# Token rows in their own segment's step, heads in two halves: a recurrent attention loop that streams its weights

## The chip, the cores and the metric

The kernel runs on one core of a Trainium2 chip. Its metric is the device time of one execution in microseconds (us). The core has a matrix engine (PE, whose weight loads are told apart as PEld), a vector engine (DVE), a scalar engine (ACT), GpSimd (POOL) and SyncE (SP), and 16 DMA engines that all DMA queues share. Each engine works through its own list of instructions in order and waits on semaphores. Here SP issues the weight loads, POOL and ACT issue the other transfers of this part.

## The reference

Two independent parts are computed and put side by side. Part A is attention with a recurrent memory, part B a long convolution by FFT (part B's code is the same in both kernels). Part A, cut to what matters:

```python
# x: (1, 2048, 1024), mem0: (1, 8, 1024); 32 heads of 128; 64 segments of 32 tokens
mem = mem0
for s in range(n_seg):
    h = concatenate([mem, xs], axis=1)          # 8 memory rows + 32 token rows
    q, k, v = h @ Wq, h @ Wk, h @ Wv            # each 1024 x 4096
    scores = where(mask, q k^T * scale, -1e9)   # memory rows see all, tokens see causally
    o = softmax(scores) v
    o = einsum('bhte,hed->btd', o, Wo)          # 4096 x 1024
    mem = o[:, :M, :]                           # the next segment's memory
    outs.append(o[:, M:, :])                    # this segment's output
```

Only the 8 memory rows go from one segment to the next. All values are bf16.

## The kernel before, in words

Part B runs first, then `part_a`. The four weight matrices of part A are 64 units of 128 x 2048 bf16 (512 KB each): 8 chunks of the contraction (`kc`) by two halves of the heads (`t`) for each of k, q and v, and 16 units `u` of two heads each for Wo. They do not all fit on chip. 41 units stay there (`load_res`, L92), the others are loaded anew in every step (`unit`, L97) through a pool `wst` of four buffers: `STREAM` (L43) names 3 of every 8 units of k, q and v, `STREAM_O` (L44) 5 of the 16 of Wo. SP issues these loads in the order of use; the load for a buffer waits until PE has read the unit that was in it.

A prologue (L105 to L165) transposes x and projects the last 8 token rows of every segment, since 8 + 32 = 40 rows do not fit the 32-row tiles. Their k, q and v go to DRAM (`PKd`, L148 and L160) and come back segment by segment (`load_pk`). The 8 rows are called the left rows here.

The loop (L208) has 66 passes, s = -1 to 64, in manual order: the instructions stand on each engine in the order in which the code records them. Pass s works on a tile `hT` of 32 rows: the 24 other token rows of segment **s + 1** and the 8 memory rows of segment **s**. It

- projects k, q and v of these rows (`quads`, four 32-row groups of PE's columns at a time), transposes k and q (`tr`), and scores the rows that are due in pass s: memory rows of s with the token rows of s that pass s - 1 prepared (L316), and the left rows (L318);
- takes the softmax of all heads at once on DVE and ACT (`softmax_a`, `softmax_b`, `ptrans`), spreads the memory rows' probabilities into block form (`blocks`, L330, DVE) and forms probabilities times v (`pv`, L344), copied to `oT` (L345);
- projects with Wo: L353 for the 32 rows of `oT` (memory rows of s, token rows of s), and L358 a second pass over the same units for the left rows `oTL` of s - 1. `po` goes to `osb` (L371), its memory rows are transposed into the next `hT` (L379, L380);
- finishes the token rows' and left rows' probabilities on POOL and DVE beside that, for the next pass (L361 to L384), and stores the output of s - 1 in eight small DMAs from POOL (L388, L389).

Of the kernel before, what the change touches and what calls it, by code (L numbers as in the profile page):

```python
# [17 lines left out]
NEG = -1.0e9  # L18
# [5 lines left out]
def part_a(ctx, tc, x, mem0, Wq, Wk, Wv, Wo, seg_len, out_a):  # L24
# [12 lines left out]
    scale = float(E ** -0.5)  # L37

# [4 lines left out]
    STREAM = {(m, t, kc) for m in "kqv" for t in range(2) for kc in (2, 5, 7)}  # L43
    STREAM_O = (2, 5, 8, 11, 14)  # L44
# [8 lines left out]
    wres = ctx.enter_context(tc.tile_pool(name="a_wres", bufs=1))  # L53
    wst = ctx.enter_context(tc.tile_pool(name="a_wst", bufs=4))
    dram = ctx.enter_context(tc.tile_pool(name="a_dram", bufs=1, space=bass.MemoryType.DRAM))
    XTd = dram.tile([NS, 128, KC * XM], BF16, name="XTd")
    PKd = dram.tile([NS, 128, 768], BF16, name="PKd")

    ctx.enter_context(tc.manual_schedule())

    ident = const.tile([128, 128], BF16, name="a_ident")
    make_identity(nc, ident[:])
    maskS = const.tile([128, NK], BF16, name="maskS")
    maskL = const.tile([128, NK], BF16, name="maskL")
    nc.gpsimd.memset(maskS[:], 0.0)
    nc.gpsimd.memset(maskL[:], 0.0)
# [4 lines left out]
    mmem = const.tile([128, 1], F32, name="mmem")  # L71
    mx_ = const.tile([128, 1], F32, name="mxx")
    nc.gpsimd.memset(mmem[:], 1.0)
    nc.gpsimd.memset(mx_[:], 1.0)
    for g in range(4):
        p = slice(32 * g, 32 * g + 32)

        def keep(t, base, cm, pattern, fill):
            nc.gpsimd.affine_select(out=t, in_=t, compare_op=ALU.is_ge, fill=fill, base=base, pattern=pattern, channel_multiplier=cm)
        keep(maskS[p, 0:XM], 0, 1, [[-1, XM]], NEG)  # L80
        keep(maskS[p, SL:NK], -XM, 1, [[0, XL]], NEG)
        keep(maskL[p, SL:NK], 0, 1, [[-1, XL]], NEG)
        keep(mmem[p, :], -XM, 1, [[0, 1]], 0.0)
        keep(mx_[p, :], XM - 1, -1, [[0, 1]], 0.0)
# [7 lines left out]
    def load_res(key):  # L92
        t_ = wres.tile([128, 2048], BF16, name="W_%s" % "_".join(str(i) for i in key))
# [11 lines left out]
    with tc.tile_pool(name="a_pxl", bufs=1) as pxl, \  # L105
# [56 lines left out]
        for u in range(16):  # L162
            if u not in STREAM_O:
                load_res(("o", u))
        pro_cm.__exit__(None, None, None)  # L165

    pers = ctx.enter_context(tc.tile_pool(name="a_pers", bufs=1))
    ld = ctx.enter_context(tc.tile_pool(name="a_ld", bufs=2))
    work = ctx.enter_context(tc.tile_pool(name="a_work", bufs=1))
    ps_acc = ctx.enter_context(tc.tile_pool(name="a_acc", bufs=2, space=PSUM))  # L170
    ps_tr = ctx.enter_context(tc.tile_pool(name="a_tr", bufs=2, space=PSUM))
    ps_att = ctx.enter_context(tc.tile_pool(name="a_att", bufs=3, space=PSUM))
    ps_o = ctx.enter_context(tc.tile_pool(name="a_o", bufs=1, space=PSUM))

    KT = pers.tile([128, 8, 4, NK], BF16, name="KT")
    QT = pers.tile([128, 8, 4, SL], BF16, name="QT")
    V = [pers.tile([128, 8, 128], BF16, name=f"V{i}") for i in range(2)]
    oT = pers.tile([128, 8, 4, SL], BF16, name="oT")
    oTL = pers.tile([128, 8, 4, XL], BF16, name="oTL")
    for t_ in (KT, QT, oT, oTL):  # L180
        nc.vector.memset(t_[:], 0.0)

    po = ps_o.tile([128, 2, 256], F32, name="po", tag="po")
    nc.vector.memset(po[:], 0.0)

    def load_pk(j):
        pk = ld.tile([128, 768], BF16, name="pk", tag="pk")
# [3 lines left out]
    def load_xt(j):  # L191
        xt = ld.tile([128, KC, XM], BF16, name="xt", tag="xt", bufs=1)
# [574 lines left out]
```

## Time and profile before

| what | value |
|---|---|
| three runs | 4604.3, 4592.44, 4604.17 us (median 4604.17) |
| profiled execution | 4595.0 us, its span 4593.3 us |
| PE busy, share of the span | 3077.3 us, 67% |
| DVE, ACT, POOL busy | 1597.9, 1325.4, 890.2 us |
| part B, up to about | 1367 us |
| part A's prologue | 1367 to 1744 us |
| the loop of 66 passes | 1744 us to the end |
| mean granted TensorE clock | 0.812 |
| `wst` loads | 1513 of 512 KB each |

The page gives busy time by engine, the span in 40 slices, the DMA queues, the chain of work that ended last, the costliest groups of instructions with the idle time before them and what ended it, and the DMA issues with their time to landing. A table by stage (busy times of a window) has these columns after the window: its length, PE, PEld, DVE, ACT and POOL busy with the count of instructions, the granted clock (PEclk), the DMA engines' share and GB/s. A row of the timeline has start, duration, engine, line, operation, output<-inputs, shape and count, and in brackets the idle time of the engine before it and what ended it.

### The profile page before, as it was taken

To read this page: it belongs to the slowest core of one execution; us is meant where nothing else is said; L and a number is where in the kernel's file an instruction comes from. 1 tells how busy PE (TensorE), PEld (TensorE's weight loads), DVE (VectorE), ACT (ScalarE), POOL (GpSimd) and SP (SyncE) were. 2 spreads that over 40 slices of the span, in tenths; PEclk is the share of its full clock that TensorE was granted. 3 is DMA by queue.
4 is the path that set the end of the run, shared out by engine and by line. 5 is a ranking of instruction groups with operands and counts; after the bars stand their busy time and mean duration, and the time that the engine had idled before them with its cause. 6 is when DMAs were issued, how large, how long until landed. Compare 5 with 4: busy or idle time off the path is not lost.

```text
span 4593.3 us, 101731 instructions
## 1 busy us (share of the span) xinstructions
PE 3077.3 (67%) x44894; PEld 1597.2 (35%) x44990; DVE 1597.9 (35%) x2887; ACT 1325.4 (29%) x1962; POOL 890.2 (19%) x1493
## 2 busy tenths in 40 slices
PE   5555543499994675766777667666666766676666
PEld 2333322244432222333333333333333333333333
DVE  8888889543001111222222222222222222222221
ACT  7999999400000001111111111111111111111111
POOL 0000000033110041222222222222222222222222
PEclk8677765699996888788787878887888888878888
DMA  3111100443233547888888888888888888888887
GB/s 112 62 62 62 62 37 6 112 152 126 87 96 117 152 149 261 272 294 285 276 285 271 301 270 289 293 281 283 281 282 295 287 278 293 281 281 299 275 291 243
DMA packets 400811, 969.45 MB, mean 211 GB/s; under 512 B 108512, under 2 KB 117728, under 8 KB 400368
## 3 DMA queue, kind: packets, MB, share of 16 engines
q1 hardware_dynamic: 330144, 923.01, 59.1%
q0 software_dynamic: 26624, 24.18, 1.7%
q10 hardware_dynamic: 43600, 15.75, 1.4%
q8 instruction: 351, 5.75, 0.5%
q14 instruction: 92, 0.75, 0.0%
HBM read 898.72 MB, written 64.04 MB: 210 GB/s over the span
## 4 chain that ended last, share of the span: by engine, by line
PE 37%; DMA 36%; ACT 11%; DVE 10%; issue 3%; POOL 1%; SPq 0%; ACTq 0%; POOLq 0%; DVEq 0%
DMA wst<-in_A_Wv_dram 11%; DMA wst<-in_A_Wq_dram 11%; DMA wst<-in_A_Wk_dram 10%; PE acc L222 7%; PE po L353 6%; PE po L358 6%; PE yp L687 5%; PE Kc L657 3%; PE Ks L658 2%; DVE lb L282 2%; PE pk_l L156 2%; DMA PKd<-kst 2%; ACT sn L407 1%; DMA xb<-in_A_x_dram 1%; ACT E L532 1%
## 5 line engine op out<-in xcount | busy, mean ns | idle before, releaser
L222 PE MATMUL acc<-wst,hT 128*32 128x512 bf16 x4680 | 542.4, 450 | 658.8 <-DMA wst<-in_A_Wk_dram 269.6
L222 PEld LDWEIGHTS <-hT 128*32 128x32 bf16 x12480 | 368.9, 103 | 1253.8 <-issue 1084.6
L228 ACT CAST qk<-acc 128x512 bf16<-128x512 f32 x195 | 114.3, 586 | 1150.6 <-PE acc L222 1150.6
L353 PE MATMUL po<-W_o,oT 128*32 128x256 bf16 x5720 | 423.0, 320 | 29.8 <-ACT oT L345 29.5
L358 PE MATMUL po<-W_o,oTL 128*8 128x256 bf16 x5632 | 416.3, 318 | 0.6 <-ACT oTL L384 0.4
L561 PE MATMUL kps<-Fr,Gr 128*64 128x17 bf16 (+1 forms) x2048 | 119.9, 198 | 301.6 <-DVE Fr L554 301.4
L353 PEld LDWEIGHTS <-oT 128*32 128x32 bf16 x8320 | 252.7, 113 | 163.0 <-ACT oT L345 92.5
L222 PE MATMUL acc<-W_q,hT 128*32 128x512 bf16 x2600 | 286.4, 507 | 0.0
L228 DVE CAST qk<-acc 128x512 bf16<-128x512 f32 x65 | 45.0, 692 | 631.8 <-PE acc L222 631.8
L200 POOL COPY KT<-pk 128x256 bf16<-128x256 bf16 x64 | 25.1, 392 | 1226.5 <-PE sc L248 1224.2
L222 PE MATMUL acc<-W_v,hT 128*32 128x512 bf16 x2600 | 256.3, 434 | 0.0
L358 PEld LDWEIGHTS <-oTL 128*8 128x8 bf16 x8192 | 221.2, 100 | 43.8 <-issue 2.0
L222 PE MATMUL acc<-W_k,hT 128*32 128x512 bf16 x2600 | 221.3, 395 | 15.5 <-POOL hT L197 15.5
L561 PEld LDWEIGHTS <-Gr 128*64 128x64 bf16 x2048 | 108.0, 144 | 345.8 <-DVE Fr L554 305.6
L657 PE MATMUL Kc<-KT,Mc 128*128 128x512 bf16 (+1 forms) x544 | 207.4, 381 | 17.0 <-DMA KT<-Kdram 15.8
L388 POOL DMA_DIRECT2D out_dram<-osb x256 | 135.8, 531 | 395.4 <-DVE osb L371 382.7
L687 PE MATMUL yp<-Ycs,Mci 128*128 128x512 bf16 (+1 forms) x543 | 207.2, 382 | 5.5 <-DMA Mci<-Mdram 3.5
L658 PE MATMUL Ks<-KT,Ms 128*128 128x512 bf16 (+1 forms) x523 | 199.1, 381 | 0.0
L687 PE MATMUL yp<-Ycs,Msi 128*128 128x512 bf16 (+1 forms) x523 | 199.0, 381 | 0.1
L353 PE MATMUL po<-wst,oT 128*32 128x256 bf16 x2600 | 195.4, 315 | 0.1
L604 PE MATMUL Us<-u_sb,Ms 128*128 128x512 bf16 (+1 forms) x520 | 168.0, 422 | 40.7 <-ACT Ms L592 32.5
L373 ACT CAST osb<-po 128x256 bf16<-128x256 f32 x64 | 23.8, 372 | 583.5 <-DVE osb L371 583.5
(201 smaller groups left out, 5738.0 us busy)
## 6 DMA issues: line engine op xcount, KB each, us to landing
wst<-in_A_Wk_dram SPq DMA_DIRECT2D x396, 512.0 KB, 5.9
wst<-in_A_Wq_dram SPq DMA_DIRECT2D x396, 512.0 KB, 6.0
wst<-in_A_Wv_dram SPq DMA_DIRECT2D x396, 512.0 KB, 5.9
wst<-in_A_Wo_dram SPq DMA_DIRECT2D x325, 512.0 KB, 5.6
Udram<-Ucs SPq DMA_DIRECT2D x32, 512.0 KB, 2.7
Ucs<-Udram SPq DMA_DIRECT2D x32, 512.0 KB, 3.7
pk<-PKd POOLq DMA_DIRECT2D x64, 192.0 KB, 6.1
Mdram<-Ms SPq DMA_DIRECT2D x17, 544.0 KB, 2.7
```

The costliest lines, as they stand in the source:

```text
L156: nc.tensor.matmul(pk[:], lhsT=us[kc][:, 512 * g + 128 * hl:512 * g + 128 * hl + 128], rhs=xTl[:, kc, :, :].rearrange("p s k -> p (s k)"), ...
L222: nc.tensor.matmul(a[32 * g:32 * g + 32, :], lhsT=hT[:, kc, :], rhs=w[:, 512 * g:512 * g + 512], start=(kc == 0), stop=(kc == KC - 1), til ...
L228: (nc.scalar.copy if eng == "a" else nc.vector.tensor_copy)(out=q[:], in_=a[:])
L282: eng.tensor_tensor(out=lb[:], in0=bc(pl[:, t, q0:q1].unsqueeze(1), [128, 16, n]), in1=bc(BDL[:].rearrange("p a b -> p (a b)").unsqueeze(2 ...
L353: nc.tensor.matmul(po[32 * qt:32 * qt + 32, 0, :], lhsT=oT[:, th, g, :], rhs=w[:, 1024 * hh + 256 * qt:1024 * hh + 256 * qt + 256], start= ...
L358: nc.tensor.matmul(po[32 * qt:32 * qt + XL, 1, :], lhsT=oTL[:, th, g, :], rhs=w[:, 1024 * hh + 256 * qt:1024 * hh + 256 * qt + 256], start ...
L388: nc.gpsimd.dma_start(out=out_a[r0:r0 + XM, 256 * qt:256 * qt + 256], in_=osb[32 * qt:32 * qt + XM, 0, :])
L561: nc.tensor.matmul(kps[pp0:pp0 + 64, dd, 0:ncol], lhsT=Gr[:, dd, :], rhs=Fr[:, dd, par_i:I:2], start=True, stop=False, tile_position=(0, p ...
L604: nc.tensor.matmul(Us[0:MM, :], lhsT=Ms[:, lc, 0:MM], rhs=u_sb[:, lc, dsl], **st)
L657: nc.tensor.matmul(Kc[0:MM, :], lhsT=Mc[:, lc, 0:MM], rhs=KT[:, lc, dsl], **st)
L658: nc.tensor.matmul(Ks[0:MM, :], lhsT=Ms[:, lc, 0:MM], rhs=KT[:, lc, dsl], **st)
L687: nc.tensor.matmul(yp[:], lhsT=Mx[0:KK, X, :], rhs=Ycs[0:KK, X, comp, dsl], start=(i_mm == 0), stop=(i_mm == n_mm - 1))
```

## The change

- **Token rows ride in their own segment's step.** There are 64 steps. `hT` of step s holds the 24 token rows and the memory rows of the same segment s; there is no pass -1 and no last pass, and no V, KT and oT that live on into the next step.
- **Heads in two halves.** q, k and v of heads half 0 are projected, scored and put through softmax while the weights of half 1 are used, and the reverse. A score tile holds a half's 32 rows and its left rows side by side, with one mask tile (`scores`, `softmax_a`, `soft_blocks`).
- **44 units kept.** 2 units of each of k0, q0, k1, q1, v0, 3 of v1 and 7 of Wo are streamed: 20 instead of 23. The kept Wo units have a pool of their own (`wreso`), which opens when the prologue's tiles are closed.
- **Left rows at the end.** Their outputs before Wo go to DRAM in each step (`OLd`); after the loop all 16 units of Wo are loaded again and the left rows of all segments are projected in one go, 256 matmuls with 512 columns.
- `warm(...)` issues nothing, since `WARM` and `TAIL` are 0.

```diff
+    STREAM = {("k", 0): (0, 4), ("q", 0): (0, 4), ("k", 1): (0, 4), ("q", 1): (0, 4), ("v", 0): (0, 4), ("v", 1): (0, 3, 6)}
+    STREAM_O = (0, 2, 5, 7, 9, 12, 14)
-    STREAM = {(m, t, kc) for m in "kqv" for t in range(2) for kc in (2, 5, 7)}
-    STREAM_O = (2, 5, 8, 11, 14)
...
+    wreso = ctx_w.enter_context(tc.tile_pool(name="a_wreso", bufs=1, side="right"))
+    for u in range(16):
+        if not streamed(("o", u)):
+            load_res(("o", u), wreso)
...
+        def soft_blocks(t, ex):
+            softmax_b(ex)
+            pt, pl = ptrans(t, ex)
+            pb = work.tile([128, 4, 4, SL], BF16, name="pb", tag="QT%d" % t)
+            lb = work.tile([128, 16, SL], BF16, name="lb", tag="KT%d" % t)
+            blocks(nc.vector, pt[:, 0:4, :], pl[:, 0, :], SL, pb[:], lb[:])
+            return pt, pl, pb, lb
...
+        a = quads("k", 0, range(KC))
+        k0 = evac(a, "qk")
+        KT0 = new_kt(0)
+        a = quads("q", 0, range(KC))
+        q0 = evac(a, "qk")
+        p0 = new_tr()
+        tr(p0, 0, k0, KT0[:, :, :, 0:SL])
+        a = quads("k", 1, H0)
+        QT0 = new_qt(0)
+        tr(p0, 1, q0, QT0[:], nc.scalar.copy)
+        quads("k", 1, H1, a)
+        k1 = evac(a, "qk")
+        KT1 = new_kt(1)
+        sc0 = scores(0, QT0, KT0)
+        ex0 = softmax_a(sc0)
+        a = quads("q", 1, range(KC))
+        q1 = evac(a, "qk")
+        p1 = new_tr()
+        tr(p1, 0, k1, KT1[:, :, :, 0:SL])
+        S0 = soft_blocks(0, ex0)
+        a = quads("v", 0, H0)
+        QT1 = new_qt(1)
+        tr(p1, 1, q1, QT1[:], nc.scalar.copy)
+        quads("v", 0, H1, a)
+        V0 = evac(a, "V0")
+        sc1 = scores(1, QT1, KT1)
+        ex1 = softmax_a(sc1)
+        L0 = left_blocks(0, S0)
+        a = quads("v", 1, H0)
+        o0 = pv_x(0, S0, V0)
+        quads("v", 1, H1, a)
+        V1 = evac(a, "V1")
+        if s + 1 < NS:
+            put_xt(xt)
...
+        S1 = soft_blocks(1, ex1)
+        L1 = left_blocks(1, S1)
+        po = ps_o.tile([128, 256], F32, name="po", tag="po")
+        oproj(po, range(0, 8), o0)
+        o1 = pv_x(1, S1, V1)
+        pl_ = ps_att.tile([128, 2, 4, 32], F32, name="pvl", tag="att")
+        pv(pl_[:, 0], 0, V0, L0[0][:], L0[1][:])
+        pv(pl_[:, 1], 1, V1, L1[0][:], L1[1][:])
+        if s + 1 < NS:
+            pk = load_pk(s + 1)
+        oproj(po, range(8, 16), o1)
+        osb = work.tile([128, 256], BF16, name="osb", tag="osb")
+        nc.vector.tensor_copy(out=osb[:], in_=po[:])
+        oTL = work.tile([128, 2, 4, 32], BF16, name="oTL", tag="oTL")
+        nc.scalar.copy(out=oTL[:], in_=pl_[:])
...
+        nc.gpsimd.dma_start(out=OLd[s], in_=oTL[:].rearrange("p t a b -> p (t a b)"))
...
+    ctx_w.close()
...
+        for u in range(16):
+            if u in (0, 2, 4, 6):
+                b = u // 2
+                raw = ex_.tile([128, 16, 32, XL], BF16, name="olr", tag="olr")
+                nc.scalar.dma_start(out=raw[:].rearrange("p s h k -> p s (h k)"), in_=OLd[16 * b:16 * b + 16].rearrange("s p f -> p s f"))
+                for n in range(2):
+                    (nc.vector.tensor_copy if n == 0 else nc.scalar.copy)(
+                        out=ol[b][:, 16 * n:16 * n + 16, :, :], in_=raw[:, :, 16 * n:16 * n + 16, :].rearrange("p s h k -> p h s k"))
+            w = ew.tile([128, 2048], BF16, name="we", tag="we")
+            nc.sync.dma_start(out=w[:].rearrange("e (h d) -> e h d", h=2), in_=unit_src(("o", u)))
...
+        for u in range(16):
+            for hh in range(2):
...
+                for b in range(4):
+                    for n in range(2):
+                        nc.tensor.matmul(pe[b][n][:], lhsT=ol[b][:, hi, :, :].rearrange("p s k -> p (s k)"), rhs=wos[u][:, 1024 * hh + 512 * n:1024 * hh + 512 * n + 512],
+                                         start=(h == 0), stop=(h == 31))
```

Three places show how instructions moved; a row names the line, the operation, output<-input and the shape, and "x2" a repetition.

SP's weight loads of one step, before and after (`wst` is the pool of four buffers, the name behind the arrow the matrix in DRAM):

```order
L101 DMA wst<-in_A_Wk_dram 128x2048 x6
L101 DMA wst<-in_A_Wq_dram 128x2048 x6
L101 DMA wst<-in_A_Wv_dram 128x2048 x6
L101 DMA wst<-in_A_Wo_dram 128x2x1024 x5
L101 DMA wst<-in_A_Wk_dram 128x2048 x6
```

```order
L100 DMA wst<-in_A_Wk_dram 128x2048 x2
L100 DMA wst<-in_A_Wq_dram 128x2048 x2
L100 DMA wst<-in_A_Wk_dram 128x2048 x2
L100 DMA wst<-in_A_Wq_dram 128x2048 x2
L100 DMA wst<-in_A_Wv_dram 128x2048 x5
L100 DMA wst<-in_A_Wo_dram 128x2x1024 x7
```

The order by matrix became an order by half, with fewer loads of k, q and v and more of Wo.

DVE between the transposed k and q (`KT`, `QT`) and the blocks (`pb`, `lb`), before and after:

```order
L241 COPY QT<-tr 128x16x8 x2
L254 TENSOR_REDUCE mx<-sc 128x8
L255 TENSOR_TENSOR sc<-sc,mx 128x320
L324 SCALAR_TENSOR_TENSOR V_13916<-acc,mmem,V_13916 128x512
L262 TENSOR_REDUCE ss<-ex 128x8
L264 RECIPROCAL rs<-ss 128x8
L265 TENSOR_TENSOR ex<-ex,rs 128x320
L327 SCALAR_TENSOR_TENSOR V_13916<-acc,mmem,V_13916 128x512
L269 STREAM_TRANSPOSE pt<-ex 128x256
L271 STREAM_TRANSPOSE pl<-ex 128x64
L277 TENSOR_TENSOR pb<-pt,BD 128x256
L282 TENSOR_TENSOR lb<-pl,BDL 128x128 x2
```

```order
L227 COPY KT<-tr 128x16x32
L252 TENSOR_REDUCE mx<-sc 128x8
L253 TENSOR_TENSOR sc<-sc,mx 128x320
L227 COPY KT<-tr 128x16x32
L260 TENSOR_REDUCE ss<-ex 128x8
L262 RECIPROCAL rs<-ss 128x8
L263 TENSOR_TENSOR ex<-ex,rs 128x320
L267 STREAM_TRANSPOSE pt<-ex 128x256
L269 STREAM_TRANSPOSE pl<-ex 128x64
L273 TENSOR_TENSOR pb<-pt,BD 128x512
L274 TENSOR_TENSOR lb<-pl,BDL 128x512
L252 TENSOR_REDUCE mx<-sc 128x8
```

The two waits for v (L324, L327) are gone from inside the softmax; the copy of the second half's k stands there instead, and the second half's softmax begins in the last row.

ACT behind the loop, which before ended with the last pass (`olr` is a block of left outputs as it lies in DRAM, `ol` the same in the order of the matmuls, `oel` the output):

```order
L375 CAST oT<-pv 128x16x24
L382 CAST oT<-pv 128x16x24
L384 CAST oTL<-pv 128x256
L373 CAST osb<-po 128x256
L762 UNCONDITIONAL_BRANCH
```

```order
L372 CAST oTL<-pvl 128x256
L395 DMA olr<-OLd 128x16x256
L397 COPY ol_50015<-olr 128x2048
L395 DMA olr<-OLd 128x16x256
L397 COPY ol_50016<-olr 128x2048
L395 DMA olr<-OLd 128x16x256
L397 COPY ol_50017<-olr 128x2048
L395 DMA olr<-OLd 128x16x256
L397 COPY ol_50018<-olr 128x2048
L414 CAST oel<-pe_50067 128x512
```

Each load of a block stands behind the copy of the block before it.

More of the change, by code (lines that the diff above doesn't have):

```diff
@@ L37, in part_a @@
     scale = float(E ** -0.5)
+    WARM = 0
+    TAIL = 0
     W3 = {"k": Wk.rearrange("(kc p) he -> kc p he", p=128),
@@ L171, in part_a @@
[L171 to L179, printed above, removed]
@@ new lines, in new_tr, with new_kt, scores @@
+        def new_tr():
+            return ps_tr.tile([128, 2, 4, 4, SL], BF16, name="tr", tag="tr")
+        def new_kt(t):
+            k = work.tile([128, 4, 4, NK], BF16, name="KT", tag="KT%d" % t)
+            nc.gpsimd.tensor_copy(out=k[:, :, :, SL:NK], in_=kl[:, t])
+            return k
+        def scores(t, QT, KT):
+            sc = ps_att.tile([128, 2, 4, NK], F32, name="sc", tag="att")
+            nc.tensor.matmul(sc[:], lhsT=ident[:], rhs=mask[:].unsqueeze(2).to_broadcast([128, 2, 4, NK]), start=True, stop=False, skip_group_check=True)
+            for hl in range(4):
```

303 lines of the change are left out of this document (119 added, 184 removed).

## The prediction

> **What bounds the kernel now.** I read the page first (span, the 40 slices, the costliest groups, the DMA issues), then tables by stage, then the timeline of one step.
>
> ```profile
> span 4593.3 us, 101731 instructions
> DMA  3111100443233547888888888888888888888887
> L222 PE MATMUL acc<-wst,hT 128*32 128x512 bf16 x4680 | 542.4, 450 | 658.8 <-DMA wst<-in_A_Wk_dram 269.6
> wst<-in_A_Wk_dram SPq DMA_DIRECT2D x396, 512.0 KB, 5.9
> ```
>
> From slice 16 on the DMA engines are 80% busy, and PE's longest idle time (658.8 us) stands before matmuls on `wst`, the streamed weights. The table by stage gives the recurrent loop: first the pass s=-1, then 64 steps, then the last pass. The columns after the length are busy times, PEclk, DMA share and GB/s.
>
> ```profile
> 1744.00:1773.00 29.00, 18.71 (x204) 7.15 (x205) 0.69 (x1) 3.96 (x8) 1.83 (x4) 0.79 0.80 261
> 1773.00:4573.70 2800.70, 1932.79 (x35829) 1024.32 (x35825) 693.01 (x1663) 459.33 (x1015) 680.51 (x1195) 0.83 0.84 285
> 4573.70:4593.30 19.60, 8.62 (x276) 7.16 (x274) 0.84 (x2) 1.79 (x5) 8.13 (x16) 0.82 0.30 96
> ```
>
> 2800.7/64 = 43.8 us a step, in which 285 GB/s x 43.8 = 12.47 MB move; 23 streamed units of 512 KB (0.524 MB) are 12.06 of them. Where in a step does the DMA stand still? The first row below is from a step's start to its output projection, the next two are that projection; then the weight phases of two other steps, and one short stretch at the best rate.
>
> ```profile
> 2960.00:2993.30 33.30, 19.43 (x291) 8.18 (x288) 8.31 (x19) 5.96 (x13) 8.20 (x16) 0.88 0.93 318
> 2993.30:2997.00 3.70, 3.70 (x72) 2.68 (x76) 1.90 (x6) 0.44 (x1) 1.85 (x4) 0.50 0.07 24
> 2997.00:3003.20 6.20, 6.20 (x195) 5.04 (x188) 0.00 (x0) 0.00 (x0) 0.16 (x1) 0.85 0.73 236
> ...
> 2650.00:2684.50 34.50, 22.44 (x372) 10.03 (x361) 6.25 (x17) 6.23 (x14) 6.03 (x13) 0.86 0.92 304
> 3442.60:3475.00 32.40, 18.56 (x286) 7.35 (x284) 8.02 (x19) 5.70 (x13) 7.87 (x14) 0.92 0.94 327
> ...
> 2988.00:2993.30 5.30, 1.25 (x18) 0.57 (x17) 4.73 (x11) 1.44 (x3) 3.69 (x6) 0.88 0.96 354
> ```
>
> While q, k and v are projected, 304 to 327 GB/s flow and PE waits for weights. Then the DMA stops (24 GB/s), and the projection is PE's own (busy in all of 3.70 and of 6.20 us). The timeline shows why:
>
> ```profile
> 2988.83 0.40 PE L222 MATMUL acc<-wst,hT 128*32 128x512 bf16 x4 [1.92 <-DMA wst<-in_A_Wv_dram]
> 2992.56 0.27 PE L293 MATMUL pv<-lb,pk 128*128 128x128 bf16 x1 [0.62 <-DVE lb L282]
> 2992.86 0.37 ACT L345 CAST oT<-pv 128x256 bf16<-128x256 f32 x1 [2.11 <-PE pv L293]
> 2993.29 0.41 PE L353 MATMUL po<-W_o,oT 128*32 128x256 bf16 x4 [0.46 <-ACT oT L345]
> 2994.97 0.43 PE L353 MATMUL po<-wst,oT 128*32 128x256 bf16 x4
> 2996.08 0.37 SPq L101 DMA_DIRECT2D wst<-in_A_Wo_dram  x1
> ```
>
> The last streamed v unit is used at 2988.83. Then softmax's blocks, pv and oT must end before unit 0 of Wo can start (2993.29) and unit 2, the first streamed one, is reached (2994.97). All four weight buffers are full by then; the next load goes out at 2996.08. So a step is 33.3 us at about 318 GB/s and 10 us of a projection that starves the DMA and does two passes (L353 and L358) over Wo.
>
> **The change: streaming.** 44 resident units of 64 leave 20 to stream. That takes 3 x 0.524 = 1.573 MB off a step; the left rows' oT to DRAM adds 0.066 and their 4 KB output pieces go (0.016): 12.47 - 1.57 + 0.05 = 10.95 MB. If the DMA no longer starves, a step is 10.95 MB / 318 GB/s = **34.4 us**. Bounds: at 354 GB/s 30.9 us, at the loop's mean of 285, 38.4 us.
>
> **Does the chain still starve it?** The heads' first half is scored after k1, and its pv sits inside v1; the second half is scored after v0, and its pv comes after eight Wo units. What a half's softmax takes is bounded from both sides by:
>
> ```profile
> 2992.43 0.48 DVE L254 TENSOR_REDUCE mx<-sc 128x8 f32<-128x320 f32 x1
> ...
> 2995.67 0.20 DVE L271 STREAM_TRANSPOSE pl<-ex 128x64 bf16<-128x64 bf16 x1
> ...
> 2989.28 0.75 DVE L327 SCALAR_TENSOR_TENSOR V<-acc,mmem,V 128x512 bf16<-128x512 f32 x1 [0.47 <-PE acc L222]
> ...
> 2990.76 1.75 DVE L282 TENSOR_TENSOR lb<-pl,BDL 128x128 bf16<-128x128 bf16 x2
> ```
>
> Maximum to last transpose is 2995.87 - 2992.43 = 3.4 us. Then come pb and lb, now 128x512 each: 0.75 us each as L327's 128x512, or 3.5 us each if they run like L282's 128x128 (0.87, beside POOL's blocks) in four times the size. With pv and oT (0.3 + 0.6) and handoffs of 0.5 that is 6.3 to 11.8 us. I take 6.3: POOL's blocks shrink to 128x128. The cover: between the second scores and its pv PE uses 3 streamed v units and 4 of Wo, 7 x 0.524 MB / 318 GB/s = 11.5 us; for the first half 2 of q, 2 of v, 2 of v1, 9.9 us. Even 11.8 leaves at most 1.9 us, less than the 4.9 us of three units in flight, so the DMA need not stop. I cost both halves at nothing; without the cover each would cost what the stall costs now, 2993.29 - 2989.23 = 4.1 us.
>
> **PE and the tail.** PE's floor follows from these rows:
>
> ```profile
> 2960.07 0.61 PE L222 MATMUL acc<-W_k,hT 128*32 128x512 bf16 x8
> 2960.51 0.39 PE L222 MATMUL acc<-wst,hT 128*32 128x512 bf16 x4
> 2960.73 0.60 PE L222 MATMUL acc<-W_k,hT 128*32 128x512 bf16 x8
> ...
> 3003.21 0.42 DVE L371 CAST osb<-po 128x256 bf16<-128x256 f32 x1 [7.34 <-PE po L358]
> ...
> 3004.56 0.61 PE L222 MATMUL acc<-W_k,hT 128*32 128x512 bf16 x8
> ```
>
> From 2960.07 to 2960.73 three units pass: 0.22 us each at full clock. 48 units are 10.6 us, and 16 of Wo, one pass, 3.5. The busy time of the first stage, 19.43 x 0.88 clock = 17.1, less 10.6, leaves 6.5 for transposes, scores and pv; I take 5 to 6.5, because the last record of each run counts the pipeline too (0.39 us for a unit that costs 0.22). Together 19 to 20.6 us, below 34.4. ACT takes over all six evacuations and half of the transposes' copies; it was busy 459.33/64 = 7.2 us a step and gives up the V and KT copies for them, so it stays far below 34.4 too. The removed L358 pass thus pays only by no longer starving the DMA. The tail from the last projection to the next k stays: 3004.56 - 3003.21 = 1.35 us, covered by three units in flight. POOL's queue after it holds five issues instead of eight, then the copies of kl; scores wait for these, three projections later. The single pk buffer is refilled before the second half of Wo, and k0, q0, k1 cover it.
>
> **Outside the steps.**
>
> ```profile
> 1741.30 0.59 DVE L181 MEMSET KT<- 128x640 uint32 x1 [10.99 <-DMA PKd<-vst]
> 1744.62 1.05 PE L222 MATMUL acc<-W_k,hT 128*32 128x512 bf16 x8 [15.04 <-POOL hT L197]
> ...
> W_o<-in_A_Wo_dram SPq DMA_DIRECT2D x11, 512.0 KB, 11.2
> PKd<-kst ACTq DMA_DIRECT2D x4, 2048.0 KB, 19.8
> ...
> 1140.00:1360.00 220.00, 219.01 (x973) 91.94 (x991) 1.00 0.28 89
> ...
> L408 ACT ACTIVATE gf_kM<-gf_nr 128x1568 f32<-128x1568 f32 x64 | 96.5, 1507 | 0.2
> ```
>
> *Start.* The Wo units now wait for the last PKd writes (1741.3), and k0's first unit, now a streamed one, queues behind nine of them on SP: ten units at 318 GB/s are 16.5 us, so the loop starts at 1741.3 + 16.5 + a landing of about 2, 1760, instead of 1744.6: **+16** (0 if the loads slip ahead, 20 at 285 GB/s). The pass s=-1 (29 us) and the last one go.
>
> *End.* 16 Wo units (8.4 MB) and four blocks of left outputs (4.2 MB) are loaded: 39.6 us at 318 GB/s. On ACT the blocks run in series (load, copy, next load; a copy of 2048 is 1507 x 2048/1568 = 2.0 us), and the first contraction needs all four. A block is 2048 pieces of 512 B; by L160's `kst` row (8192 pieces of 256 B in 19.8 us) it takes 5 us by pieces or 10 by bytes, twice that beside the weights: the last is ready 29 to 73 us after the loop. I take 40, the bytes' own time. Then 256 matmuls 128x512 at 220/973 = 0.226 us: 58 us, and 5 for copies and stores: **103** (92 to 136). The Trainium skill ("DMA: Bandwidth & Descriptors", the quick-reference figures) puts line rate at pieces of 512 B and more; by it a block at 318 GB/s is 3.3 us and the sum is some 11 us shorter than mine, by `kst`'s rate in bytes it would be longer.
>
> *Sum.* 1744.6 + 16 + 64 x 34.4 (2202) + 103 = 4066 us of span against 4593.3. The profiled execution took 4595.0, 1.7 more than its span, and the three runs shown have a median of 4604.2, 9 more: **4070 us**.
>
> **Rivals.** (B) The starving moves rather than ends: a tail, pv in mid-stream and k0 again hold all four buffers, and the mean stays 285 GB/s: 38.4 us a step, 4070 + 64 x 4.0 = 4326. For it speaks that no weight phase is above 0.96 DMA share; against, that what stops the DMA today is one place. (C) Without the stop the rate is that of 2988 to 2993, 354 GB/s: 30.9 us, 4070 - 224 = 3846. Against: three steps' weight phases give 304 to 327. (E) PE becomes the bound at half clock: the rows at 0.50 (2993.3 to 2997.0) show it after a wait. Then 19 to 20.6 become 38 to 41 us, with the tail some 40.9: 4070 + 64 x 6.5 = 4486. Against: the granted clock is 0.83 over the loop with the same kind of waits, and a PE that is always busy got 1.00 (1140 to 1360). The Trainium skill ("TensorE: Matmul & The Clock Gate", "HAM oscillation — how this bites in real kernels") says that compute bursts shorter than the waits for weights start cold every time; the loop's mix of 0.50 and 1.00 agrees in part, so E keeps a chance. (D, slower) Token rows in their own step make the step one serial path: PE at half clock (38 us), the tail, and both halves uncovered (2 x 4.1): 47.7 us, 4070 + 64 x 13.3 = 4921. It decides from (4593 - 1744.6 - 16 - 103)/64 = 42.6 us a step. Against: 9.9 and 11.5 us of streamed work lie between.
>
> **How the numbers follow.** Forecast 0.65 (steps of 32.2 to 36.5 us, 3930 to 4205), B 0.14, C 0.13, E 0.05, D 0.03. The range takes in B and part of C: 3900 to 4335. The measurement tells 0.3% (14 us) from no change; E's upper end touches it: faster 0.96, same 0.01, slower 0.03.
>
> **What would show it.** Right: in the profile after, 20 `wst` loads and 34 to 35 us a step, a DMA share above 0.9 without a stretch near zero, PE's waits still on `wst`, the first po matmul of a step waiting under 1 us for oT, PEclk above 0.7. An end of 95 to 115 us whose first contraction waits for the last `ol`. Wrong: PE waiting for DVE's lb or ACT's oT (the cover failed), PEclk near 0.5 (E), steps below 32 us (C), or an equal DMA share with fewer bytes (B).

## The result, and the profile after

| what | before | predicted | after |
|---|---|---|---|
| median of three runs, us | 4604.17 | 4070 (3900 to 4335) | 3976.45 (3972.9 to 3979.72) |
| ratio to before, 95% interval | 1 | 0.884 | 0.8644 (0.862 to 0.8667) |
| profiled execution, its span | 4595.0, 4593.3 | span 4066 | 3979.72, 3978.0 |
| loop starts at | 1744.6 | 1760 | 1749.2 |
| a step, mean | 43.8 | 34.4 (32.2 to 36.5) | 33.2 |
| after the last step's `osb` | | 103 (92 to 136) | 104 |

The forecast's case came true, 94 us faster than its number. The rows below are the page of the changed kernel: span, DMA engines in 40 slices, PE's longest idle time, DMA issues. The second fence is the table by stage for 1500 us of the loop.

```profile
span 3978.0 us, 82935 instructions
DMA  3111111034423334369999999999999999999993
L215 PE MATMUL acc<-wst,hT 128*32 128x512 bf16 x3328 | 350.6, 408 | 352.9 <-DMA wst<-in_A_Wv_dram 118.3
wst<-in_A_Wk_dram SPq DMA_DIRECT2D x260, 512.0 KB, 5.8
```

```profile
2000.00:3500.00 1500.00, 1067.16 (x19096) 530.72 (x19096) 436.25 (x991) 314.83 (x586) 329.84 (x634) 0.89 0.95 328
```

From the 19th slice to the last but one the DMA engines are at 9 tenths, where they were at 8. 328 GB/s flow, where the loop's mean was 285. PE still waits for streamed weights (352.9 us before these matmuls), so the steps are still bound by the stream; it only no longer stops. The traces also hold every DMA packet, the piece that a DMA engine moves at a time. Counted from these between 2000 and 3500 us, no packet at all is under way for 4.7% of the time in the kernel before, and for 0.0% in the changed one. The chain that used to stop it, now in the timeline of one step:

```profile
2936.97 0.59 ACT L298 CAST oT<-pv 128x512 bf16<-128x512 f32 x1 [7.33 <-PE pv L280]
2937.61 0.62 PE L315 MATMUL po<-W_o,oT 128*32 128x256 bf16 x8 [0.30 <-ACT oT L298]
2940.84 0.42 DVE L370 CAST osb<-po 128x256 bf16<-128x256 f32 x1 [10.33 <-PE po L315]
2941.64 0.19 DVE L378 COPY hT<-tro 128x64 bf16<-128x64 bf16 x1 [0.38 <-PE tro L377]
2941.89 0.40 PE L215 MATMUL acc<-wst,hT 128*32 128x512 bf16 x4 [0.28 <-DVE hT L378]
2943.56 0.53 POOL L234 COPY KT<-pk 128x128 bf16<-128x128 bf16 x2
2952.08 0.28 PE L242 MATMUL sc<-KT,QT 128*32 128x40 bf16 x16
...
2957.39 0.67 DVE L273 TENSOR_TENSOR pb<-pt,BD 128x512 bf16<-128x512 bf16 x1
2962.73 0.68 DVE L274 TENSOR_TENSOR lb<-pl,BDL 128x512 bf16<-128x512 bf16 x1
2963.62 0.40 PE L315 MATMUL po<-wst,oT 128*32 128x256 bf16 x8 [0.70 <-DMA wst<-in_A_Wo_dram]
```

In brackets stand the idle time before an instruction and its cause. `oT` lets PE idle 0.30 us instead of 0.46 behind a 4 us chain; 26 us later, in the next step, the projection on half 0 waits for a transfer, not for `oT`. Over 2070 us of the loop, the waits (in total, times, longest) read:

```profile
PE po L315 <- DMA wst<-in_A_Wo_dram: 224.2, 271, 2.9
PE acc L215 <- DMA wst<-in_A_Wv_dram: 115.0, 154, 2.8
PE acc L215 <- DMA wst<-in_A_Wq_dram: 105.3, 146, 2.5
PE acc L215 <- DMA wst<-in_A_Wk_dram: 80.8, 83, 2.3
PE tro L377 <- DVE osb L370: 33.1, 62, 0.5
PE po L315 <- ACT oT L298: 20.7, 62, 0.4
```

The first four are the stream. The softmax's last product, `oT`, costs 20.7 us in 62 steps.

### The profile page after: what moved, and what is told of

Its sections match the earlier page's. It is cut to its first block, busy times and chain, and to the rows that moved or that the text cites. A ratio compares the mean times of both kernels' runs of the same rounds, so it can differ in the third digit from the quotient of the medians.

```text
span 3978.0 us, 82935 instructions
## 1 busy us (share of the span) xinstructions
PE 2688.7 (68%) x36078; PEld 1331.3 (33%) x36078; DVE 1524.4 (38%) x2632; ACT 1320.4 (33%) x1779; POOL 667.1 (17%) x1162
## 4 chain that ended last, share of the span: by engine, by line
DMA 45%; PE 32%; ACT 13%; DVE 5%; issue 2%; POOL 1%; SPq 0%; ACTq 0%; DVEq 0%; POOLq 0%
DMA wst<-in_A_Wo_dram 13%; DMA wst<-in_A_Wq_dram 12%; DMA wst<-in_A_Wv_dram 11%; PE acc L215 7%; PE yp L714 6%; PE po L315 4%; DMA wst<-in_A_Wk_dram 3%; PE Kc L684 3%; PE Ks L685 3%; PE pk_l L155 3%; DMA PKd<-kst 2%; DMA xb<-in_A_x_dram 2%; ACT E L559 2%; ACT sn L434 1%; POOL PKd L147 1%
## 5 line engine op out<-in xcount | busy, mean ns | idle before, releaser
L215 PE MATMUL acc<-wst,hT 128*32 128x512 bf16 x3328 | 350.6, 408 | 352.9 <-DMA wst<-in_A_Wv_dram 118.3
L215 PEld LDWEIGHTS <-hT 128*32 128x32 bf16 x12288 | 315.5, 99 | 728.6 <-issue 383.8
L221 ACT CAST qk<-acc 128x512 bf16<-128x512 f32 x256 | 149.8, 585 | 801.1 <-PE acc L215 786.0
L227 DVE COPY KT<-tr 128x512 bf16<-128x512 bf16 x128 | 54.3, 424 | 608.6 <-PE tr L226 608.6
L315 PE MATMUL po<-W_o,oT 128*32 128x256 bf16 x4608 | 258.4, 327 | 21.4 <-ACT oT L298 21.4
L370 DVE CAST osb<-po 128x256 bf16<-128x256 f32 x64 | 27.1, 424 | 621.2 <-PE po L315 621.2
L215 PE MATMUL acc<-W_q,hT 128*32 128x512 bf16 x3072 | 236.8, 414 | 0.0
L273 POOL TENSOR_TENSOR pbl<-pt,BD 128x128 bf16<-128x128 bf16 x128 | 87.9, 687 | 870.6 <-DVE pt L267 865.3
L298 ACT CAST oT<-pv 128x512 bf16<-128x512 f32 x128 | 74.9, 585 | 460.1 <-PE pv L280 459.8
L215 PE MATMUL acc<-W_v,hT 128*32 128x512 bf16 x2816 | 216.6, 391 | 0.0
```

The costliest lines, as they stand in the source:

```text
L215: nc.tensor.matmul(a[32 * g:32 * g + 32, :], lhsT=hT[:, kc, :], rhs=w[:, 512 * g:512 * g + 512], start=(kc == 0), stop=(kc == KC - 1), til ...
L221: nc.scalar.copy(out=q[:], in_=a[:])
L273: eng.tensor_tensor(out=pb, in0=bc(pt.unsqueeze(2), [128, 4, 4, n]), in1=bc(BD[:].unsqueeze(1).unsqueeze(3), [128, 4, 4, n]), op=ALU.mult)
L315: nc.tensor.matmul(po[32 * qt:32 * qt + 32, :], lhsT=oT[:, h % 4, (h % 16) // 4, :], rhs=w[:, 1024 * hh + 256 * qt:1024 * hh + 256 * qt + ...
```

## The experiments

All times are medians beside runs of the kernel before on the same chip, all ratios are to that kernel. Edits are to the changed kernel unless the text says otherwise.

### What the 10.6 us of a step are made of

*Three more units streamed* (`stream23`): 41 kept and 23 streamed, as before, in the new order.

```diff
-    STREAM = {..., ("q", 0): (0, 4), ..., ("q", 1): (0, 4), ("v", 0): (0, 4), ...}
+    STREAM = {..., ("q", 0): (0, 3, 6), ..., ("q", 1): (0, 3, 6), ("v", 0): (0, 3, 6), ...}
```

> The changed kernel with 41 units kept and 23 streamed, as many as in the kernel before (one more of each of q0, q1 and v0). Theory (bytes over the DMA rate set the step): 3 x 0.524 MB at the 327 GB/s of the changed kernel's loop are 4.8 us a step, 33.2 becomes 38.0 and the whole 3978 + 64 x 4.8 = 4285 us. Rival (the recurrence or PE sets the step, the weights are hidden): within 20 us of 3978.

Measured: 4277.92 us, 0.9296 (0.9259 to 0.9333); 38.1 us a step.

```profile
2000.00:3500.00 1500.00, 998.55 (x16711) 467.66 (x16711) 374.38 (x863) 276.19 (x513) 283.58 (x552) 0.87 0.95 328
```

The rate is the same 328 GB/s to the digit, and the time follows the bytes: 301 us in 64 steps are 4.7 us a step, 1.573 MB / 328 GB/s = 4.8. No weight load is hidden for free; this theory stood.

*Before without its second pass* (`before_one_pass`), an edit to the kernel before: the pass over Wo for the left rows (L358) runs for the last head only, so the left rows' outputs lack the other heads.

```diff
-                    if s >= 1:
+                    if s >= 1 and h == 31:
                         for qt in range(4):
                             nc.tensor.matmul(po[32 * qt:32 * qt + XL, 1, :], ...
```

> The kernel before without the second pass over Wo (L358), so the left rows' outputs are left out except for the last head. Theory (PE's two passes at half clock starve the DMA after the softmax stall): the projection took 9.9 us and 16 units at 0.43 us are 6.9, so a step loses 3.0 us, 4595 - 192 = 4403 us; the DMA's stop before it stays. Rival (the pass lay beside transfers that had to come anyway): within 30 us of 4595.

Measured: 4399.62 us, 0.9566 (0.9521 to 0.961); 40.6 us a step, 3.1 less, as expected. In the order of before, these matmuls stood in the stretch where the DMA starved, and cost their own time.

*Softmax late* (`late_softmax`): both halves are scored after v0, and both halves' pv stand behind all of v1, ahead of Wo. Nothing else is changed.

```diff
-        sc0 = scores(0, QT0, KT0)
-        ex0 = softmax_a(sc0)
         a = quads("q", 1, range(KC))
...
-        S0 = soft_blocks(0, ex0)
         a = quads("v", 0, H0)
...
+        sc0 = scores(0, QT0, KT0)
         sc1 = scores(1, QT1, KT1)
+        ex0 = softmax_a(sc0)
+        a = quads("v", 1, range(KC))
+        V1 = evac(a, "V1")
+        S0 = soft_blocks(0, ex0)
+        L0 = left_blocks(0, S0)
         ex1 = softmax_a(sc1)
-        L0 = left_blocks(0, S0)
-        a = quads("v", 1, H0)
-        o0 = pv_x(0, S0, V0)
-        quads("v", 1, H1, a)
-        V1 = evac(a, "V1")
...
-        oproj(po, range(0, 8), o0)
+        o0 = pv_x(0, S0, V0)
         o1 = pv_x(1, S1, V1)
+        oproj(po, range(0, 8), o0)
```

> The changed kernel with the interleaving undone: both halves are scored after v0 and v1 is all that is left between the scores and the first Wo unit. Theory (a wait costs only what it lasts beyond the three or four units in flight): two softmax chains of some 5 us in series and pv and oT, less the 4.8 us of v1's three units, leave PE a wait of 6 to 7 us, of which the DMA covers 5 to 6; with a restart of about 2 us the step grows by 1.5 to 3 us: 4075 to 4170 us. Rival 1 (the interleaving brings nothing, fewer bytes and one pass over Wo are all): 3978 to 4000. Rival 2 (each uncovered half costs the 4.1 us that the stall cost before): +8.2 us a step, 4500.

Measured: 4251.88 us, 0.9241 (0.9203 to 0.9279); 37.6 us a step, 4.3 more. It lies above the theory's range and below the second rival. Its timeline, its waits and its table by stage:

```profile
3012.78 0.40 PE L215 MATMUL acc<-wst,hT 128*32 128x512 bf16 x4 [0.45 <-DMA wst<-in_A_Wv_dram]
3018.86 0.58 PE L278 MATMUL pv<-pb,V 128*128 128x128 bf16 x4 [3.61 <-DVE pb L273]
3020.09 0.62 PE L315 MATMUL po<-wst,oT 128*32 128x256 bf16 x8
...
3031.37 0.62 PE L215 MATMUL acc<-wst,hT 128*32 128x512 bf16 x4 [1.92 <-DMA wst<-in_A_Wk_dram]
```

```profile
PE pv L278 <- DVE pb L273: 274.2, 112, 3.7
```

```profile
2000.00:3500.00 1500.00, 1007.36 (x16961) 486.43 (x16960) 389.48 (x888) 280.39 (x522) 318.04 (x563) 0.82 0.84 292
3016.00:3020.50 4.50, 1.51 (x17) 0.75 (x21) 3.15 (x7) 0.96 (x3) 1.94 (x3) 0.50 0.33 117
```

From the last v (3012.78 + 0.40) to the first Wo (3020.09) it is 6.9 us, which the expectation had. In this stop the rate is down to 117 GB/s (3016.0 to 3020.5), and over 1500 us it falls to 292 GB/s at a share of 0.84, close to the 285 and 0.84 of the loop before. The theory's error was to let the transfers cover 5 to 6 of the 6.9: in this trace no DMA packet is under way for 7.1% of the time, 2.7 us a step. The rest of the 4.3 is argued: the stream also has to start up again, and PE then waits for k0 (1.92 us in the last row of the timeline). So a stop of this length, behind all buffers full, costs about 4.3 us a step, and the interleaving is worth that.

Together: 4.7 for the bytes (stream23), 3.1 for the second pass (before_one_pass), and the remaining 2.8 of 10.6 for the stop. The last is a remainder; putting a stop back into the new order cost 4.3. With that the three prices add up to 12.1, 1.5 us too much: they were measured in two different orders, and the stop's share is known only as 2.8 to 4.3 us.

### Are small DMAs or POOL's queue in the way?

*Each output stored twice to the same place* (`outs8`):

```diff
+            for _ in range(2):
+                nc.gpsimd.dma_start(out=out_a[...], in_=osb[...])
-            nc.gpsimd.dma_start(out=out_a[...], in_=osb[...])
```

> The changed kernel with its four output DMAs of a step issued twice (eight, as many as before). Theory (only bytes count, and the 318 GB/s of the kernel before held the ramp after its stop): 0.05 MB a step at 327 GB/s are 0.15 us, 3978 + 10 = 3988 us. Rival (the small output DMAs from POOL lower the rate, 318 against 327 GB/s): +0.9 us a step, 4035 us.

Measured: 4562.39 us, 0.9921 (0.9894 to 0.9947); 42.4 us a step, 9.2 more. Both expectations missed it. Waits and timeline:

```profile
POOL out_dram L384 <- DMA out_dram<-osb: 891.1, 245, 7.0
PE sc L242 <- POOL KT L234: 568.0, 63, 11.8
```

```profile
3020.10 1.01 POOL L384 DMA_DIRECT2D out_dram<-osb  x2 [4.37 <-DMA out_dram<-osb]
...
3033.66 0.53 POOL L234 COPY KT<-pk 128x128 bf16<-128x128 bf16 x2
3034.01 0.33 PE L242 MATMUL sc<-KT,QT 128*32 128x40 bf16 x16 [9.07 <-POOL KT L234]
```

POOL issues the second write to the same rows only when it has been told that the first has landed (the row waits on that DMA), and stands still for that, four times a step. Behind these issues stands the copy of the left rows' k (L234), and PE's scores wait 9 us for it. The experiment thus priced something else than it was meant to: the slack of POOL's queue. In the changed kernel this copy ends at 2944.1 and the scores start at 2952.08, 8 us later; what POOL is late beyond that, every step pays.

*The same four extra DMAs to another place* (`outs_scratch`), so that nothing has to wait:

```diff
+    OXd = dram.tile([NS, 4, 24, 1024], BF16, name="OXd")
...
+            nc.gpsimd.dma_start(out=OXd[s, qt, :, 256 * qt:256 * qt + 256], in_=osb[...])
```

> The changed kernel with four more output DMAs a step, of the same form, into a place of their own in DRAM that nothing else writes, so that none waits for another (unlike the run with the outputs written twice, where POOL waited for each write to land). Theory (only bytes count): 0.15 us a step, 3988 us. Rival 1 (small DMAs lower the rate, 318 against 327 GB/s): +0.9 us a step, 4035 us. Rival 2 (the four more issues on POOL, 2 us, make kl's copies late): with the 10 us of slack that the changed kernel's timeline shows before the scores, nothing.

Measured: 3975.44 us, 0.864 (0.8608 to 0.8672): the changed kernel's time. Four more small transfers a step cost nothing, and the rate does not suffer from them (330 GB/s).

### What sets the rate

The prediction treated the rate as a property of the stretch of work, and the DMA share of 0.95 reads as engines that are full. Three edits tell that apart from a rate set by the number of loads in flight. One unit of on-chip space is one buffer or one kept unit, so 3 + 45, 4 + 44 and 5 + 43 take the same space.

```diff
 bufs3
-    wst = ctx_w.enter_context(tc.tile_pool(name="a_wst", bufs=4, side="right"))
+    wst = ctx_w.enter_context(tc.tile_pool(name="a_wst", bufs=3, side="right"))
 bufs3_45: the same, and
-    STREAM = {..., ("v", 1): (0, 3, 6)}
+    STREAM = {..., ("v", 1): (0, 4)}
 bufs5
-    STREAM = {..., ("v", 0): (0, 4), ("v", 1): (0, 3, 6)}
+    STREAM = {..., ("v", 0): (0, 3, 6), ("v", 1): (0, 3, 6)}
-    wst = ctx_w.enter_context(tc.tile_pool(name="a_wst", bufs=4, side="right"))
+    wst = ctx_w.enter_context(tc.tile_pool(name="a_wst", bufs=5, side="right"))
```

> The changed kernel with three weight buffers instead of four, the same 20 streamed units. Theory (the DMA engines are full, the time to landing of 5.8 us is a queue that gets shorter with fewer in flight): at most +1.3 us a step, 3978 to 4060 us. Rival (the rate is the depth over a fixed time to landing): 20 x 5.8/3 = 38.7 us a step, 4330 us.

> Three weight buffers, and the room of the fourth for one more kept unit (45 kept, 19 streamed). Theory: 33.2 x 10.43/10.95 = 31.6 us a step and up to 1.3 for the lost depth: 3876 to 3960 us. Rival (depth over a fixed time to landing): 19 x 5.8/3 = 36.7 us, 4200 us.

> Five weight buffers and 43 kept units (21 streamed), the reverse trade to the run with three buffers and 45 kept. Theory (at four the engines are almost full, share 0.95, so a fifth can win at most 5%): 11.47 MB at 328 to 345 GB/s are 33.2 to 35.0 us a step, 3978 to 4093 us. Rival (the rate goes on growing with the depth as from three to four, 275 to 328): 5/4 x 328 = 410 GB/s, 28 us a step, 3640 us.

Measured:

| label | buffers, streamed | us | ratio | step, us | GB/s | DMA share |
|---|---|---|---|---|---|---|
| bufs3 | 3, 20 | 4395.15 | 0.9559 (0.9533 to 0.9585) | 39.76 | 275 | 0.84 |
| bufs3_45 | 3, 19 | 4263.07 | 0.9273 (0.9248 to 0.9298) | 37.54 | 276 | 0.84 |
| the change | 4, 20 | 3976.45 | 0.8644 (0.862 to 0.8667) | 33.2 | 328 | 0.95 |
| bufs5 | 5, 21 | 3781.05 | 0.8206 (0.818 to 0.8233) | 30.26 | 379 | 1.02 |

The table by stage and a row of the DMA issues (its last number is the median time from issue to landing), first of `bufs3`, then of `bufs5`:

```profile
2000.00:3500.00 1500.00, 1000.15 (x15999) 486.32 (x16002) 358.12 (x833) 263.69 (x490) 271.26 (x532) 0.80 0.84 275
```

```profile
wst<-in_A_Wv_dram SPq DMA_DIRECT2D x325, 512.0 KB, 5.3
```

```profile
2000.00:3500.00 1500.00, 1119.87 (x21063) 553.30 (x21063) 481.31 (x1094) 347.78 (x645) 367.18 (x700) 0.94 1.02 379
```

```profile
wst<-in_A_Wv_dram SPq DMA_DIRECT2D x390, 512.0 KB, 6.3
```

The theory of full engines fell with all three. In `bufs5` more bytes a step are moved in less time. The rate goes with the loads in flight: 3, 4 and 5 units over their landing time of 5.3, 6.1 (the change's row is the same line with x325 and 6.1) and 6.3 us are 297, 344 and 416 GB/s, and 93%, 95% and 91% of that was measured (of the streamed units alone, 264, 316 and 364 GB/s: 89%, 92% and 87%). Landing takes longer with depth, but by far less than in proportion, which is why the rival with a fixed landing time came near for three buffers and promised too much for five. Another reading would be that deeper buffers only bridge stops of the stream. The packets of the traces speak against it: in bufs3, the change and bufs5 a packet is under way practically all the time (none for 0.02%, 0.00% and 0.00% of 1500 us), and fewer than eight at once are for 4.3%, 0.6% and 0.0%, while the rate differs by 16 to 19% from one depth to the next. One kept unit given up for a buffer gains 195 us, though it adds 0.524 MB to every step.

The share misleads: from bufs3 to bufs5 the rate rises by 38%, the share by 21% (0.84 to 1.02). Busy time per byte falls with depth, so a share of 0.95 was no ceiling. Why a byte takes the engines less time with more loads in flight stays open; no run here was made for it. The Trainium skill ("DMA: Bandwidth & Descriptors", Specifications) gives a limit of about 358 GB/s for a core's memory, half of what two cores share; its section Bandwidth says that this is a core's part when both stream. This program runs on one core, and its 379 GB/s, of which the streamed units alone are 364 (21 x 0.524 MB in 30.26 us), show that 358 is no limit here.

### The left rows at the end

The end stage of the changed kernel, from the last loads of Wo to the last of the four blocks:

```profile
3874.15 31.64 SPq L400 DMA_DIRECT2D we<-in_A_Wo_dram  x16
3882.12 1.90 ACT L397 COPY ol<-olr 128x2048 bf16<-128x2048 bf16 x1 [10.95 <-DMA we<-in_A_Wo_dram]
3893.58 1.90 ACT L397 COPY ol<-olr 128x2048 bf16<-128x2048 bf16 x1 [9.56 <-DMA olr<-OLd]
...
3912.68 1.90 ACT L397 COPY ol<-olr 128x2048 bf16<-128x2048 bf16 x1 [5.35 <-DMA olr<-OLd]
...
3913.43 55.59 PE L409 MATMUL pe<-we,ol 128*128 128x512 bf16 x250 [6.21 <-DVE ol L397]
```

Load and copy alternate; the fourth copy starts at 3912.68, 39 us after the loop, and 250 of PE's 256 matmuls start only behind it.

*Blocks first* (`end_first`): all four blocks are loaded by SP ahead of the Wo units, the copies follow.

```diff
+        for b in range(4):
+            raw = ex_.tile([128, 16, 32, XL], BF16, name="olr", tag="olr", bufs=4)
+            nc.sync.dma_start(out=raw[:].rearrange("p s h k -> p s (h k)"), in_=OLd[16 * b:16 * b + 16].rearrange("s p f -> p s f"))
+            raws.append(raw)
...
-            if u in (0, 2, 4, 6):
-                raw = ...; nc.scalar.dma_start(out=raw...); (copies)
+        for b in range(4): (the same copies, from raws[b])
```

> The changed kernel with the stage behind the loop in another order: all four blocks of left outputs are loaded first, on SP ahead of the 16 Wo units, and copied afterwards. Theory (the end's 104 us are 40 us until the last block is in place, because the blocks run in series on ACT and share the DMA with Wo, and 58 of PE): 4.2 MB at 327 GB/s are 13 us, with start and copies 20: the end takes 82 us, 3956 us. Rival (pieces of 512 B are slow by themselves, 10 us a block): 3975 us.

Measured: 3941.33 us, 0.8574 (0.8558 to 0.8589). The last `osb` is at 3855.4 and the span ends at 3937.4: 82.0 us instead of 104, as expected. The rest of the 35 us is a slightly shorter step.

*Back into the loop* (`left_in_loop`): the left rows go through Wo one step later beside the 32 rows, as before, in the new order; there is no `OLd`, and in place of the end stage one pass over Wo for the last segment's left rows.

```diff
-        def oproj(po, us, oT):
+        def oproj(po, us, oT, oL):
...
+                    if oL is not None:
+                        for qt in range(4):
+                            nc.tensor.matmul(po[32 * qt:32 * qt + XL, 1, :], lhsT=oL[...], rhs=w[...],
+                                             start=False, stop=(h == 31), tile_position=(0, 32 * qt), ...)
...
+            osl = work.tile([128, 256], BF16, name="osl", tag="ex")
+            nc.scalar.copy(out=osl[:], in_=po[:, 1, :])
-        nc.gpsimd.dma_start(out=OLd[s], in_=oTL[:].rearrange("p t a b -> p (t a b)"))
+        oL = oTL
```

> The changed kernel with one part undone: the left rows go through Wo in the loop again, in a second pass over each unit for the step before, and the stage behind the loop is a single pass over Wo for the last segment. Theory (PE's 20 us a step plus 3.5 for the second pass still lie under the 33.2 us of the weights, with no stall ahead of them): the step stays, the end falls from 104 to some 15 us, 3889 us. Rival (the second pass keeps buffers from being freed and starves the DMA as it did before, where leaving it out won 3.1 us a step): 3889 + 64 x 3.1 = 4087 us.

Measured: 3855.14 us, 0.8366 (0.8344 to 0.8388), better than the theory.

```profile
2000.00:3500.00 1500.00, 1145.84 (x25436) 655.59 (x25425) 444.19 (x1012) 339.62 (x644) 406.56 (x782) 0.98 0.95 334
```

PE does the added matmuls under the transfers: the step is 32.6 us, not longer but 0.6 shorter, and from the last `osb` (3835.5) to the end it is 20 us instead of 104. 84 + 64 x 0.6 = 122 us, about the 121 gained. So this part of the change cost time. The second pass that took 3.1 us a step before is free here. That fits a price that came from the stop ahead of it and not from its matmuls; no run has the pass and the stop together in the new order.

### The clock

*Warm-up matmuls on* (`warm2`): the kernel's own `warm(...)` issues them again at its places.

```diff
-    WARM = 0
+    WARM = 2
```

> The changed kernel with two idle matmuls of 512 columns in front of each streamed unit (WARM = 2), 8.6 us more of PE a step, which keep its clock up (now 0.89 in the loop). Theory (the weights set the step and PE has room): 3960 to 4000 us. Rival 1 (PE's half clock late in the step costs time): faster by 1% or more, under 3940. Rival 2 (what delays the release of a buffer costs, as depth does): 20 units later by up to 0.43 us each where PE did not wait, up to +3 us a step, 4100 to 4170.

Measured: 4014.98 us, 0.8719 (0.8699 to 0.8739); 33.7 us a step.

```profile
2000.00:3500.00 1500.00, 1384.90 (x20681) 530.03 (x20677) 423.75 (x985) 312.65 (x580) 324.44 (x624) 1.00 0.94 324
```

The clock rises from 0.89 to 1.00, and the step is 0.5 us longer. So there is no sign that the lower clock costs the changed kernel time; PE's waits are for weights. What the clock alone is worth is not separated from what the added matmuls cost: they keep PE busy for 92% of the stretch. (Whether the clock of 0.98 has a part in the shorter step of `left_in_loop` stays open too.)

### The two better parts together

`both` is `left_in_loop` with the two edits of `bufs5`.

```diff
 left_in_loop, and
-    STREAM = {..., ("v", 0): (0, 4), ("v", 1): (0, 3, 6)}
+    STREAM = {..., ("v", 0): (0, 3, 6), ("v", 1): (0, 3, 6)}
-    ... name="a_wst", bufs=4 ...
+    ... name="a_wst", bufs=5 ...
```

> Edit: five weight buffers with 43 kept units and 21 streamed (as bufs5), and the left rows' outputs back in the loop one step behind, without the end stage (as left_in_loop). Theory (the loop goes by the rate of the streamed units, which depends on how many are in flight; the left rows' matmuls in the loop ride under the transfers; the end stage only adds time behind the loop): the two gains add. bufs5 took 0.8206 and left_in_loop 0.8366 against 0.8640 of the change, 200 us and 126 us at 4604; the sum is 3976 - 200 - 126 = 3650 us, a step of about 29.6 us, ratio 0.793. If the lower clock of bufs5 (0.94) rises as it did in left_in_loop, slightly below. Rival 1 (TensorE becomes the bound: 1145.84 us of busy time in 1500 with 32.59 us steps is 24.9 us a step, and each wait for the scores comes on top, so that steps shorter than 30.3 us are not reached with the 512 further matmul records of the left rows): the step stays at bufs5's 30.26 us and only the end is saved, 3781 - 85 = about 3696 us. Rival 2 (the second pass at each unit slows the release of the buffers again, as in the kernel before): the step becomes longer, over 32 us, 3800 us or more.

Measured: 3695.12 us, 0.8015 (0.7995 to 0.8035); 30.19 us a step. That is 909 us less than the kernel before and 281 less than the change. Table by stage and PE's three largest waits in it:

```profile
2000.00:3500.00 1500.00, 1224.03 (x27412) 697.32 (x27413) 478.83 (x1087) 364.31 (x693) 445.12 (x848) 0.99 1.01 377
```

```profile
PE po L318 <- DMA wst<-in_A_Wo_dram: 73.3, 147, 1.5
PE acc L218 <- DMA wst<-in_A_Wv_dram: 68.7, 120, 1.9
PE acc L218 <- DMA wst<-in_A_Wq_dram: 29.0, 71, 1.9
```

The time is that of rival 1 (3696): only the end is saved, the step stays that of `bufs5` (30.26). Its reason is not borne out: PE is busy for 82% of the stretch and still waits 73.3 + 68.7 + 29.0 us for weights there. The bytes and the rate are those of `bufs5`, and these alone give the step. Why the 0.6 us that the same edit saved with four buffers are missing with five stays open, as does whether a sixth buffer would raise the rate again; neither was tried.

## Why the prediction was right, and where it was off

- **What bounds it: right.** The stream bounds the step, its stop could be removed, and bytes over rate gives the time. `stream23` moved the bytes alone and the time followed; `late_softmax` put a stop alone back, and with 292 GB/s nearly the old rate came back. Of the 10.6 us gained the stop is one part of three. What the prediction did not ask is what sets the rate when nothing stops; the number of buffers does, and one more gained another 195 us.
- **The step, 34.4 us: too long by 1.2,** and outside the "34 to 35" that was named as a sign of being right. The bytes were right (10.95 MB; 328 GB/s x 33.2 us = 10.9). The mis-sized term is the 318 GB/s, taken from 2960.0 to 2993.3 of the kernel before. The first 7 us of that stretch are the start after the stop:

```profile
2960.00:2967.00 7.00, 3.42 (x55) 1.41 (x53) 0.00 (x0) 1.20 (x3) 4.12 (x9) 1.00 0.86 275
2967.00:2988.00 21.00, 14.77 (x218) 6.19 (x218) 3.59 (x9) 3.32 (x8) 0.39 (x1) 0.84 0.94 323
```

Without them, 323 over 21 us and 354 over 5.3 us are 329 GB/s, the changed kernel's 328. Four other steps cut the same way have 275 to 314 GB/s in their first 7 us and 328, 311, 331 and 328 behind them (2264.2 to 2289.9, 2657.0 to 2684.5, 3449.6 to 3475.0, 4013.0 to 4040.0). A stretch without the stop should have been cut behind the restart. This is 77 of the 88 us by which the span was overstated.
- **The chain costs nothing: right.** pb and lb take 0.68 and 0.89 us in the median of 128 (0.75 each was taken, against a bound of 3.5; the timeline above shows a short lb), and the first po matmul waits 0.3 us for oT. The stream never stands still. The price without the cover, 4.1 us for each half, was too high for the two together: uncovered in one stop they cost 4.3.
- **PE's floor of 19 to 20.6 us: nearly right.** 1067.16 us x 0.89 in 1500 / 33.2 = 45.2 steps are 21.0 us.
- **POOL's five issues ahead of the kl copy, "three projections later": right,** with 8 us to spare; `outs8` showed what is late when the spare is used up.
- **Start, +16: it was +4.6.** The queue of ten units took about as long as worked out, 17.2 us from the first `W_o` load to the first matmul against 18.5. But it began nine us before the 1741.3 that was taken from the old trace:

```profile
1732.05 5.36 SPq L93 DMA_DIRECT2D W_o<-in_A_Wo_dram  x9
1749.20 0.62 PE L215 MATMUL acc<-wst,hT 128*32 128x512 bf16 x4 [26.09 <-DMA wst<-in_A_Wk_dram]
```

The term that failed is the old end of the PKd writes as the new start: the last of them is issued at 1730.1 instead of 1739.3. Before, eleven W_o loads went out from 1680.9, amid these writes; now a single weight load does (1677.7). That this is why the writes end earlier fits both traces, and no run tried it alone.

- **End, 103: 104.** The chain of four blocks was as described and the last one was ready 39 us after the loop (40 taken). In these 38.5 us the DMA moves 321 GB/s, so the bytes' own time was the right choice. The first blocks landed about 11.4 us after their issue, the last 7.1, all beside Wo units. The 3.3 us worked out beside it from the Trainium skill ("DMA: Bandwidth & Descriptors", Specifications: line rate at pieces of 512 B and more) agree with neither. What the prediction did not ask is whether the stage pays at all: it costs 84 us more than the same work in the loop.
- **The rivals.** B (285 GB/s) and D need a stop that is no longer there; `late_softmax` shows that B's mechanism is real. C (354 GB/s) was not reached with four buffers. E fell: the clock was 0.89, PE's own work 21.0 us of a 33.2 us step, and a full clock (`warm2`) did not shorten it. The Trainium skill's rule ("TensorE: Matmul & The Clock Gate", "HAM oscillation — how this bites in real kernels") is about idle gaps of PE of more than some 3.4 us, a condition that the prediction left out. The longest wait for weights in the table above is 2.9 us; the mean clock is below full all the same, so the trace agrees only in part, and the time does not hang on it.
- **Slips in the sums.** By its own terms the start is 1741.3 + 16.5 + 2 - 1744.6 = 15 us (17 at 285 GB/s, not 20), four blocks at twice 10 us and 2 for each copy are 88 us and not 73, and 4066 + 1.7 + 9 is 4077 and not 4070. None of them moves the measured time out of the range.

## What to carry to other kernels

When a loop streams its weights, measure the rate at two buffer depths before taking it as given: a DMA share of 0.95 did not mean that the engines were full, and a kept unit traded for a fifth buffer gained 195 us. Take a rate from a stretch that begins behind the restart after a stop. Before work is moved out of such a loop, ask what it waits for there: here the left rows' matmuls cost nothing under the transfers, and behind the loop 84 us.

## What was not expected of the hardware

- The rate of 512 KB loads on one queue rises with the loads in flight, 275, 328 and 379 GB/s for 3, 4 and 5, while the busy share goes from 0.84 to 1.02, above one.
- POOL issued a second write to the same rows of DRAM only after the first had landed; with four pairs a step that was 9.2 us a step, through one engine's queue. Whether the hardware needs that order, no run shows: the wait is one of the program.
- Four more small stores a step, independent of each other, cost nothing measurable (3975.44 against 3976.45 us).
